# A three-stage kernel on one core: the written-out order of its first half, arranged anew

## The chip, the core and the metric

The kernel runs on one core of a Trainium2 chip. The metric is device time in microseconds (us) for one execution of the whole program, lower is better. The engines are named as the profile names them: PE (TensorE, with PEld for its weight loads), DVE (VectorE), ACT (ScalarE), POOL (GpSimd) and SP (SyncE, which here issues every DMA).

## What is computed

Three stages follow each other: a gated linear attention over 768 steps for 2 x 8 heads of width 40, then a gated feed-forward layer (320 to 1536 and back) with an RMS norm ahead of it, then a second feed-forward layer (320 to 2048 and back) with a leaky ReLU. All data is float32.

```
# attention, step t
m_new = max(f + m, i);  f_stab = exp(f + m - m_new);  i_stab = exp(i - m_new)
C = f_stab * C + i_stab * outer(v, k);  n = f_stab * n + i_stab * k
y[t] = sigmoid(o_gate) * (C @ q) / max(|n . q|, 1)
# first feed-forward
xn = x / sqrt(mean(x*x) + 1e-6) * rms_g
x = (silu(xn @ w_gate) * (xn @ w_val)) @ w_out
# second feed-forward
h = x @ w_in;  x = max(0.01*h, h) @ w_out2
```

## The kernel before

The 1536 tokens are 12 tiles T of 128 (chunk c = T // 2 of batch T % 2). The attention works chunk by chunk, with a state C carried from chunk to chunk; four groups g of three tiles each (0 to 2, 3 to 5, 6 to 8, 9 to 11) then go through the feed-forward layers, with 12 blocks f of 128 hidden columns in the first one. Weights and activations are split into a high and a low float32r half, and a product is summed from several matmuls.

Nothing is scheduled at build time. ORDER is a text of 1928 short steps, and play() emits the instructions of one step after the other. Each engine works off its own instructions strictly in that order, SP its DMAs too, so the text sets every queue. The steps that the prediction speaks of, with the line of their main instruction:

- sf, sa (L231, L232, L238): scans over the gates on DVE; id (L226): a matmul without use, which only keeps PE at work.
- fa.T.e (L258, L261): PE builds the decay rows A of tile T for the even or odd heads, in PSUM; arg.T.e (L351): ACT turns them into weights w by four exponentials. From tile 2 on, the rows come by DMA as Ab, and POOL masks them first (mask, L355).
- qk.T (L335): scores s on PE. p.T.e (L382): DVE multiplies scores and weights. av, inn, kv (L395, L405, L417): the attention's other matmuls, into one PSUM bank of tile T. eq, k, c (L359, L374, L364): POOL prepares operands of inn and kv and scales the state.
- y1, rec, yr, sq, y2, xn, xc (L450 to L492): the output gate and the norm; y2.T.1 (L479) is on POOL, xn (L488) on DVE. tp.T (L499) transposes on PE, xh.T (L503, ACT) and xl.T (L507, DVE) write tile T of X, the input of the first feed-forward layer.
- a, r, b (L536, L538, L540 and after): a weight block is converted in four steps that alternate between DVE and ACT. wA, wR, wB are the DMAs of it.
- U.g.f.h (L646): eight up matmuls of group g, block f, gate or value half h. T, E, M, S, L (L673 or L671, L678, L685 or L683, L694, L700): the activation, the products and the split of the result into sh and sl, on ACT and DVE. D.g.b.i (L718) and DW (L736): the down matmuls; K and KW: their sums into x2.

The PSUM banks of the attention, of the up matmuls, of the down sums and of the scores come from four pools of two banks each. Loads have two or three buffers, so a DMA on SP waits until its buffer is free, and those behind it wait too.

Group 1 cannot begin (U.1.0.0) before xl.5 has written the last of its tiles. U.1.0.0 is the 84th step on PE. The step DW.1.8 is the 193rd on PE.

Of the kernel before, what the change touches and what calls it, by code (L numbers as in the profile page):

```python
# [51 lines left out]
co.0.0.1 cv.0.0.1 cr cl r.1 fa.0.0 arg.0.0 sf.2.6 fa.1.1 uv.0.1 arg.1.1 fa.0.1 sa.2.6 uv.1.2 ux.0.1 co.1.0.1 wR.0
ug.2.6 id.1 co.0.1.2 arg.0.1 r.1 r.0 r.1 r.0 id.1 dn.2 dA.0.2 dq.1 r.0 ev.1.2 ux.2.6 ex.1.2 r.0 r.1 a.0 dn.1 cv.1.0.1
fa.1.0 arg.1.0 dn.0 th.0 eg.2.6 k.0 da.2 ex.2.6 a.0 k.1 qk.0 p.0.0 qk.1 a.0 p.1.0 av.0.0 p.0.1 av.0.1 abs.0 p.1.1
av.1.0 av.1.1 da.3 id.1 mask.2.1 cv.0.1.2 mask.2.0 co.0.2.6 dE.1.2 y1.0 id.1 arg.2.0 a.0 kv.0 abs.1 wR.2 r.2 mask.3.1
rec.0 wA.1 a.1 rec.1 r.2 dq.2 a.1 yr.0 id.1 mask.3.0 arg.3.0 r.2 id.1 r.2 qk.2 th.1 st.0 y1.1 de.2 dA.2.6 eq.2 ux.1.2
co.1.1.2 cv.1.1.2 cv.0.2.6 sq.0 y2.0.0 yr.1 wA.2 kv.1 dgb p.2.0 av.2.0 arg.2.1 y2.0.1 p.2.1 y2.0.2 k.2 sq.1 y2.1.0 a.2
y2.1.1 a.1 xn.0 a.2 arg.3.1 a.1 dq.3 qk.3 p.3.1 dq.4 cb.0 wB.1 a.2 xc.0 b.1 dsl y2.1.2 th.2 a.2 dr.2.6 da.4 mask.4.1
wA.4 xn.1 av.2.1 inn.2 y1.2 xc.1 id.1 st.1 abs.2 id.1 id.1 id.1 p.3.0 rec.2 tp.0 id.1 b.1 tp.1 dn.3 yr.2 dr.1.2
mask.4.0 dc.1.2 a.4 sq.2 b.1 y2.2.0 kv.2 xh.1 wR.3 th.3 de.3 dE.2.6 k.3 b.1 id.1 xh.0 xl.0 av.3.0 co.1.2.6 cv.1.2.6  # L60
xl.1 cb.1 y2.2.1 y2.2.2 r.3 qk.4 eq.3 av.3.1 inn.3 dv.1.2 xn.2 arg.4.0 xc.2 tp.2 abs.3 r.3 r.3 c.3 rec.3 dn.5 kv.3 a.4
xh.2 arg.4.1 xl.2 U.0.1.1 p.4.0 k.5 y1.3 da.5 a.4 st.3 U.0.1.0 cb.3 p.4.1 th.5 T.0.1 dn.4 th.4 mask.5.0 wA.3 yr.3 sq.3
a.4 E.0.1 mask.5.1 a.3 arg.5.1 dc.2.6 de.4 r.3 arg.5.0 y2.3.0 a.3 eq.4 M.0.1 av.4.0 av.4.1 inn.4 dq.5 qk.5 y2.3.1 y1.4
p.5.1 U.0.0.0 p.5.0 T.0.0 E.0.0 dv.2.6 U.0.0.1 M.0.0 da.6 mask.6.1 arg.6.1 de.5 wB.0 abs.4 dq.6 a.3 rec.4 mask.6.0
av.5.0 av.5.1 S.0.1 eq.5 y2.3.2 yr.4 S.0.0 inn.5 kv.5 abs.5 b.0 xn.3 rec.5 b.0 sq.4 y2.4.0 y2.4.1 arg.6.0 qk.6 L.0.1
p.6.1 U.0.2.0 p.6.0 U.0.2.1 T.0.2 E.0.2 c.2 y1.5 dq.7 b.0 c.5 st.5 qk.7 yr.5 y2.4.2 c.4 cb.5 sq.5 a.3 k.4 kv.4 id.1
xc.3 tp.3 xh.3 y2.5.0 y2.5.1 dq.8 xn.4 da.7 xc.4 M.0.2 wB.2 U.0.3.0 st.4 cb.4 y2.5.2 c.6 L.0.0 xn.5 xl.3 tp.4 xh.4
xl.4 U.0.3.1 S.0.2 xc.5 T.0.3 tp.5 xh.5 de.6 dn.6 av.6.0 E.0.3 xl.5 av.6.1 wB.3 M.0.3 L.0.2 eq.6 inn.6 abs.6 wA.5 b.0
b.3 U.1.0.0 T.1.0 E.1.0 U.1.0.1 M.1.0 U.1.1.0 da.8 U.1.2.0 b.3 mask.7.0 arg.7.0 p.7.0 dn.7 av.7.0 mask.7.1 arg.7.1
p.7.1 av.7.1 k.7 S.0.3 b.2 L.0.3 de.7 b.2 eq.7 S.1.0 b.2 inn.7 L.1.0 b.2 b.3 b.3 wB.4 rec.6 T.1.2 E.1.2 mask.8.1 a.5  # L70
# [1025 lines left out]
```

## Time and profile before

| | |
|---|---|
| times of three runs | 445.22, 447.4, 451.2 us; median 447.4 |
| span of the profiled execution | 449.2 us (inside the three runs' range, 1.8 above their median) |
| PE busy | 437.8 us, 97% |
| DVE, ACT, POOL busy | 365.8 (81%), 281.3 (63%), 102.1 us (23%) |
| chain that ended last | PE 89%, DVE 6%, ACT 2%, issue 2% |

A busy time is the time in which at least one instruction of the engine is under way. Matmuls overlap each other, so a stretch in which PE is busy need not be one in which it is fast. The column PEclk in the rows below is the granted TensorE clock, as a share of its upper level of 2.4 GHz; 0.5 is the lower level of 1.2 GHz.

### The profile page before, as it was taken

To read this page: it belongs to the slowest core of one execution; us is meant where nothing else is said; L and a number is where in the kernel's file an instruction comes from. 1 tells how busy PE (TensorE), PEld (TensorE's weight loads), DVE (VectorE), ACT (ScalarE), POOL (GpSimd) and SP (SyncE) were. 2 spreads that over 40 slices of the span, in tenths; PEclk is the share of its full clock that TensorE was granted. 3 is DMA by queue.
4 is the path that set the end of the run, shared out by engine and by line. 5 is a ranking of instruction groups with operands and counts; after the bars stand their busy time and mean duration, and the time that the engine had idled before them with its cause. 6 is when DMAs were issued, how large, how long until landed. Compare 5 with 4: busy or idle time off the path is not lost.

```text
span 449.2 us, 9736 instructions
## 1 busy us (share of the span) xinstructions
PE 437.8 (97%) x3720; PEld 415.7 (93%) x3720; DVE 365.8 (81%) x822; ACT 281.3 (63%) x709; POOL 102.1 (23%) x162
## 2 busy tenths in 40 slices
...
GB/s 267 316 265 283 251 287 119 265 232 82 248 88 77 56 0 175 78 83 0 124 1 1 1 1 0 1 1 153 30 31 76 107 47 32 31 29 31 0 2 176
DMA packets 21039, 45.47 MB, mean 101 GB/s; under 512 B 2128, under 2 KB 9168, under 8 KB 20992
## 3 DMA queue, kind: packets, MB, share of 16 engines
...
HBM read 42.79 MB, written 2.06 MB: 100 GB/s over the span
## 4 chain that ended last, share of the span: by engine, by line
PE 89%; DVE 6%; ACT 2%; issue 2%; DVEq 0%; ACTq 0%
PE h L796 13%; PE xa L718 10%; PE g L646 8%; PE v L646 8%; PE oa L969 6%; PE oa L968 6%; PE oa L967 6%; PE u L796 6%; PE xw L736 5%; PE s L335 3%; PE h L802 2%; PE h L801 2%; PE o L395 2%; PE busy L226 2%; PE o L405 1%
## 5 line engine op out<-in xcount | busy, mean ns | idle before, releaser
L969 PE MATMUL oa<-wB,xl 128*128 128x320 f32 x192 | 59.3, 309 | 0.0
L968 PE MATMUL oa<-wB,xh 128*128 128x320 f32 x192 | 59.3, 309 | 0.0
L967 PE MATMUL oa<-wB,xh 128*128 128x320 f32 x192 | 59.2, 308 | 0.0
L646 PE MATMUL g<-X,wA 128*128 128x384 f32 x256 | 50.7, 343 | 0.9 <-ACT th L671 0.4
L979 DVE TENSOR_TENSOR x<-oa,x 128x320 f32<-128x320 f32 x84 | 39.5, 484 | 14.6 <-PE oa L969 13.9
L646 PE MATMUL v<-X,wA 128*128 128x384 f32 x256 | 50.0, 339 | 0.1
L646 PEld LDWEIGHTS g<-X,wA 128*128 128x128 f32 x256 | 44.5, 189 | 2.9 <-ACT th L671 0.7
L718 PE MATMUL xa<-sh,wB 128*128 128x384 f32 x160 | 46.0, 338 | 0.0
L646 PEld LDWEIGHTS v<-X,wA 128*128 128x128 f32 x256 | 44.6, 188 | 0.7 <-DVE X L507 0.4
L578 POOL TENSOR_TENSOR sums<-w_A 128x128 f32<-128x128 f32 x8 | 3.9, 488 | 151.8 <-DVE w_A L540 146.6
L969 PEld LDWEIGHTS oa<-wB,xl 128*128 128x128 f32 x192 | 36.0, 188 | 0.1
L967 PEld LDWEIGHTS oa<-wB,xh 128*128 128x128 f32 x192 | 36.0, 188 | 0.0
L968 PEld LDWEIGHTS oa<-wB,xh 128*128 128x128 f32 x192 | 36.0, 188 | 0.0
L796 PE MATMUL h<-X,wA 128*128 128x384 f32 x144 | 32.2, 337 | 0.0
L718 PE MATMUL xa<-sl,wB 128*128 128x384 f32 x96 | 32.2, 336 | 0.0
L943 ACT ACTIVATE c<-c 128x384 f32<-128x384 f32 x48 | 25.2, 525 | 7.2 <-DVE c L840 3.4
L718 PEld LDWEIGHTS xa<-sh,wB 128*128 128x128 f32 x160 | 29.4, 188 | 0.1
L953 DVE TENSOR_TENSOR xl<-c,xh 128x384 fp32r<-128x384 f32 x48 | 26.1, 556 | 1.0 <-ACT xh L948 0.8
L948 ACT CAST xh<-c 128x384 fp32r<-128x384 f32 x48 | 24.3, 513 | 2.9 <-PE oa L968 2.2
L351 ACT ACTIVATE w<-Ab,aeu 128x128 f32<-128x128 f32 x80 | 25.3, 392 | 0.6 <-POOL Ab L355 0.6
L796 PEld LDWEIGHTS h<-X,wA 128*128 128x128 f32 x144 | 25.0, 188 | 0.1
L479 POOL TENSOR_TENSOR sm<-sm,mhalf 128x1 f32<-128x1 f32 x12 | 8.0, 663 | 65.0 <-DVE sm L477 65.0
...
## 6 DMA issues: line engine op xcount, KB each, us to landing
...
```

Of the source, the lines that this page charges most:

```text
L351: A.activation(w[:, j], src, AF.Exp, scale=-1.0, bias=col)
L646: PE.matmul(dst, a, x, start=(i == 0), stop=(i == len(seq) - 1))
L718: PE.matmul(xa, w, x, start=(k == 0), stop=(k == len(seq) - 1))
L736: PE.matmul(xas["w", g, i], a, x, start=(f == NE and k == 0), stop=(f == NF - 1 and k == len(seq) - 1),)
L796: PE.matmul(dst, x, y, start=first and j == 0, stop=j == 2, skip_group_check=not first)
L943: A.activation(t, src, AF.Prelu, alpha=0.01)
L948: A.copy(v["h"], v["t"])
L953: V.tensor_tensor(v["l"], v["t"], v["h"].bitcast(F32), op=ALU.subtract)
L967: PE.matmul(oa, v["h"][:, ts], wb[:, 0:DM], start=m == 0, stop=False)
L968: PE.matmul(oa, v["h"][:, ts], wb[:, DM:], start=False, stop=False)
L969: PE.matmul(oa, v["l"][:, ts], wb[:, 0:DM], start=False, stop=m == 1)
L979: V.tensor_tensor(dst, oas[k, p, i], dst, op=ALU.add)
```

## The change

Only the text ORDER differs: its first 1028 steps stand in another order, the last 900 (from S.1.11 on) are the same. Each of the 1928 steps occurs as often as before; no function and no size is touched. The text takes one line more, so that the code below it is one line further down in the changed kernel (L646 is L647 there). The first line of either text:

```diff
-id.1 id.1 id.1 id.1 did cr id.1 id.1 dfg dig id.1 id.1 id.1 wR.1 dq.0 ms id.1 sf.0.1 sa.0.1 sf.1.2 id.1 sa.1.2 wA.0
+id.1 id.1 id.1 id.1 id.1 cl wR.1 r.1 id.1 id.1 id.1 id.1 dfg ms dig sf.0.1 r.1 did cr cr co.0.0.1 id.1 id.1 sa.0.1
```

**The start on SP and DVE.** DVE before, from its first instruction on (x is the space of the gates; raw_R and w_R belong to the first weight block, wgr):

```order
L231 SCALAR_TENSOR_TENSOR x_91<-x_91 16x128
L232 TENSOR_TENSOR x_91<-x_91 16x128
L238 SCALAR_TENSOR_TENSOR x_91<-x_91 16x128
L231 SCALAR_TENSOR_TENSOR x_91<-x_91 16x128
L232 TENSOR_TENSOR x_91<-x_91 16x128
L237 COPY x_91<-x_91 16x1
L238 SCALAR_TENSOR_TENSOR x_91<-x_91 16x128
L252 COPY aeu<-pt_0_152 128x16
L536 TENSOR_SCALAR w_R_160<-raw_R_130 128x256
```

The same place now:

```order
L537 TENSOR_SCALAR w_R_124<-raw_R_122 128x256
L232 SCALAR_TENSOR_TENSOR x_91<-x_91 16x128
L233 TENSOR_TENSOR x_91<-x_91 16x128
L541 SCALAR_TENSOR_TENSOR w_R_124<-raw_R_122,w_R_124 128x256
L239 SCALAR_TENSOR_TENSOR x_91<-x_91 16x128
L232 SCALAR_TENSOR_TENSOR x_91<-x_91 16x128
L233 TENSOR_TENSOR x_91<-x_91 16x128
L238 COPY x_91<-x_91 16x1
L239 SCALAR_TENSOR_TENSOR x_91<-x_91 16x128
```

The first two steps of the conversion r.1 stand around the first scan. SP before begins with the constants, the two gate inputs and then this weight block; now:

```order
L527 DMA raw_R_122<-wgr 128x512
L994 DMA x_91<-fg 16x768
L994 DMA x_91<-ig 16x768
L995 DMA consts<-cst 128x256
L315 DMA nat_173<-nat 128x968
L996 DMA sel<-cst 16x136
L527 DMA raw_R_176<-wgr 128x512
L527 DMA raw_A_222<-wgv 128x1024
L310 DMA qkt_224<-qk 128x1024
```

The weight block goes first, the constants fourth, and the first scores' operand qkt ninth instead of fifth.

**The first scores on PE.** Before, the last of the four fa (A rows) stands just ahead of qk.0 (s is its output):

```order
L226 LDWEIGHTS const-bfloat16-1.0
L226 MATMUL busy<-const-bfloat16-1.0 128x512
L258 MATMUL A_0_246<-consts_r 128x512
L261 MATMUL A_0_246<-x_91,consts 128x128 x4
L335 MATMUL s_0_270<-qkt_132 128x128
L335 MATMUL s_1_271<-qkt_132 128x128
```

Now qk.0 follows the third fa and two small transposes:

```order
L259 MATMUL A_1_189<-consts_r 128x512
L262 MATMUL A_1_189<-x_91,consts 128x128 x4
L249 MATMUL pt_0_195<-consts,x_91 128x16
L249 MATMUL pt_1_230<-consts,x_91 128x16
L336 MATMUL s_0_232<-qkt_224 128x128
L336 MATMUL s_1_233<-qkt_224 128x128
```

The fourth fa has gone behind qk.1, and arg.1.1, which reads it on ACT, has moved back too.

**The end of group 1's attention on DVE and POOL.** DVE before, up to the write of tile 5 (xl.5, the last row; sm are the norm's columns, tp the transposed tiles):

```order
L481 TENSOR_SCALAR sm_1038<-sm_1038 128x1
L482 TENSOR_SCALAR sm_1038<-sm_1038 128x1
L483 TENSOR_TENSOR sm_1038<-sm_1038 128x1
L700 TENSOR_TENSOR sl_0_1168<-th_0_933,sh_0_1012 128x384
L488 SCALAR_TENSOR_TENSOR xn_1170<-y_1093,sm_1038,gb 128x320
L507 TENSOR_TENSOR X<-tp_1135,X 128x3x128
L507 TENSOR_TENSOR X<-tp_1173,X 128x3x128
L678 SCALAR_TENSOR_TENSOR th_3_1191<-th_3_1191,g_3_1152 128x384
L507 TENSOR_TENSOR X<-tp_1193,X 128x3x128
```

Now:

```order
L482 TENSOR_SCALAR sm_1030<-sm_1030 128x1
L483 TENSOR_SCALAR sm_1030<-sm_1030 128x1
L484 TENSOR_TENSOR sm_1030<-sm_1030 128x1
L701 TENSOR_TENSOR sl_0_1134<-th_0_961,sh_0_1067 128x384
L508 TENSOR_TENSOR X<-tp_1137,X 128x3x128
L489 SCALAR_TENSOR_TENSOR xn_1163<-y_1044,sm_1030,gb 128x320
L508 TENSOR_TENSOR X<-tp_1117,X 128x3x128
L679 SCALAR_TENSOR_TENSOR th_3_1161<-th_3_1161,g_3_1101 128x384
L508 TENSOR_TENSOR X<-tp_1181,X 128x3x128
```

One of the three writes of X has moved ahead of xn.5. POOL at that place before, from the norm's step y2.5.1 on:

```order
L479 TENSOR_TENSOR sm_1038<-sm_1038,mhalf 128x1
L364 TENSOR_TENSOR C_95<-C_95,gdec 104x164
L359 TENSOR_TENSOR eb_1198<-eb_1198,qkt_964 128x512
L355 AFFINE_SELECT Ab_1146<-Ab_1146 128x4x128 x2
L374 TENSOR_TENSOR Kt_100<-nat_1321,aeu 128x4x40 x2
```

and now:

```order
L480 TENSOR_TENSOR sm_1030<-sm_1030,mhalf 128x1
L360 TENSOR_TENSOR eb_1144<-eb_1144,qkt_1089 128x512
L375 TENSOR_TENSOR Kt_99<-nat_1157,aeu 128x4x40 x2
L365 TENSOR_TENSOR C_95<-C_95,gdec 104x164
L356 AFFINE_SELECT Ab_1278<-Ab_1278 128x4x128 x2
```

The state's scaling c.6 has moved behind eq.6 and k.6, and the two masks of tile 7 behind all of them.

Over the whole first part, the same 83 steps stand on PE ahead of U.1.0.0 in both texts, and the same 192 ahead of DW.1.8. On DVE, 121 steps end with xl.5 before and 119 now; the two that have gone behind it are the first two of the conversion b.0.

## Rows read from the trace of the kernel before

**Rows 1.** Windows: stage (from:to, length), busy us of each engine, clock, DMA.
```profile
core 0: us, PE busy (x) PEld busy (x) DVE busy (x) ACT busy (x) POOL busy (x), PEclk, DMA share, GB/s
0.00:9.40 9.40, 8.62 (x32) 4.23 (x32) 5.41 (x14) 4.01 (x10) 3.16 (x13) 1.00 0.73 246
9.40:47.48 38.08, 35.06 (x516) 26.53 (x516) 28.73 (x82) 25.99 (x83) 16.07 (x23) 0.55 0.93 288
47.48:73.65 26.17, 23.53 (x447) 20.86 (x445) 25.36 (x59) 18.02 (x55) 14.21 (x22) 0.95 0.81 260
73.65:211.26 137.61, 136.72 (x1310) 132.40 (x1307) 106.54 (x252) 82.66 (x224) 32.88 (x47) 1.00 0.37 113
211.26:449.20 237.94, 233.82 (x1425) 231.66 (x1424) 199.79 (x420) 150.60 (x341) 35.77 (x58) 1.00 0.13 41
```

**Rows 2.** Timeline of PE: tp.5 and the first up matmuls of group 1.
```profile
70.73 0.64 PE L499 MATMUL tp<-consts,xn 128*128 128x128 f32 x3 [2.49 <-DVE X L507]
73.65 2.00 PE L646 MATMUL g<-X,wA 128*128 128x384 f32 x8
75.48 1.55 PE L646 MATMUL v<-X,wA 128*128 128x384 f32 x8
76.87 3.05 PE L646 MATMUL g<-X,wA 128*128 128x384 f32 x16
```

**Rows 3.** Windows of DVE alone, cut at p.1.1, p.2.1, xl.2 and xl.5.
```profile
0.00:21.23 21.23, 12.82 (x32) 0.72 0.83 294
21.23:30.82 9.59, 7.89 (x23) 0.50 0.93 291
30.82:48.00 17.18, 13.95 (x43) 0.63 0.94 255
48.00:72.45 24.45, 23.64 (x57) 0.97 0.84 272
```

**Rows 4.** Waits of DVE until 74 us: total, times, longest.
```profile
DVE x L231 <- DMA x<-fg: 3.3, 1, 3.3
DVE w_R L540 <- ACT raw_R L538: 2.3, 1, 2.3
DVE w L382 <- PE s L335: 1.6, 2, 1.1
```

**Rows 5.** Timeline of DVE: xn and yr, each once long and once short.
```profile
66.95 3.17 DVE L488 SCALAR_TENSOR_TENSOR xn<-y,sm,gb 128x320 f32<-128x320 f32 x1
64.76 0.54 DVE L488 SCALAR_TENSOR_TENSOR xn<-y,sm,gb 128x320 f32<-128x320 f32 x1
49.76 1.58 DVE L464 TENSOR_TENSOR y<-y,sm 128x320 f32<-128x320 f32 x1
63.09 0.52 DVE L464 TENSOR_TENSOR y<-y,sm 128x320 f32<-128x320 f32 x1
```

**Rows 6.** Timeline of POOL beside the long xn.
```profile
66.79 0.58 POOL L364 TENSOR_TENSOR C<-C,gdec 104x164 f32<-104x164 f32 x1 [1.08 <-DMA raw_B<-wo]
67.32 1.28 POOL L359 TENSOR_TENSOR eb<-eb,qkt 128x512 f32<-128x512 f32 x1
68.56 1.22 POOL L355 TENSOR_SCALAR_AFFINE_SELECT Ab<-Ab 128x512 f32<-128x512 f32 x2
```

**Rows 7.** POOL groups until 74 us: k (Kt) and its mean.
```profile
L374 POOL TENSOR_TENSOR Kt<-nat,aeu 128x160 f32<-128x160 f32 x14 | 7.2, 537 | 13.4 <-DVE aeu L252 3.6 <-PE tp L499 3.6 <-PE o L417 3.2
```

**Rows 8.** Timeline, the start: second gate input, first weight block, first p.
```profile
4.16 0.28 DVE L232 TENSOR_TENSOR x<-x 16x128 f32<-16x128 f32 x1 [0.44 <-DMA x<-ig]
5.50 0.44 ACT L538 ACTIVATE raw_R<-raw_R 128x256 f32<-128x256 f32 x1 [1.70 <-DMA raw_R<-wgr]
17.55 0.69 DVE L382 TENSOR_TENSOR w<-s,w 128x512 f32<-128x512 f32 x1 [0.56 <-PE s L335]
```

**Rows 9.** Timeline of DVE: the two steps of b.0 ahead of xl.5.
```profile
58.75 0.32 DVE L536 TENSOR_SCALAR w_B<-raw_B 128x320 uint32<-128x320 uint32 x1
59.77 0.44 DVE L540 SCALAR_TENSOR_TENSOR w_B<-raw_B,w_B 128x320 uint32<-128x320 uint32 x1
```

More of the change, by code (lines that the diff above doesn't have):

```diff
@@ L50 @@
 ORDER = """
-id.1 id.1 id.1 id.1 did cr id.1 id.1 dfg dig id.1 id.1 id.1 wR.1 dq.0 ms id.1 sf.0.1 sa.0.1 sf.1.2 id.1 sa.1.2 wA.0
[L52 to L70, printed above, removed]
```

210 lines of the change are left out of this document (115 added, 95 removed).

## The prediction

> **What bounds the kernel now.** The first view is the row of windows by stage, cut at three places of PE's order: where U.1.0.0 starts (73.65), where DW.1.8 starts (211.26), and earlier where the first up matmul starts (47.48). In the last two stages PE is busy 136.72 of 137.61 us and 233.82 of 237.94 us at the full granted clock, 1.00 [rows 1]. There the kernel is bound by PE's own work; no order of the same matmuls can take more than the 0.9 us of idle time from the second last stage, and the last one keeps its order. What an order can win lies in the first 73.65 us.
>
> In that part PE isn't the bound. From 9.40 to 47.48 its granted clock is 0.55, mostly the lower level of 1.2 GHz, and DVE is busy 28.73 of 38.08 us [rows 1]. From 47.48 to 73.65 DVE is busy 25.36 of 26.17 us. U.1.0.0 at 73.65 is held up by the transposes ahead of it: tp.5 waits 2.49 us for DVE [rows 2]. So the second view is DVE alone, cut at four steps whose last one, xl.5, ends at 72.45: busy 12.82 + 7.89 + 13.95 + 23.64 = 58.3 us, idle 8.4 + 1.7 + 3.2 + 0.8 = 14.1 us [rows 3]. The third view says what the idle time waited for: 3.3 us for the first gate input, 2.3 for ACT's first step on the second weight block, 1.6 for the scores [rows 4]. The fourth is DVE's timeline, where some busy time is a wait in disguise. An xn takes 0.54 us at 64.76 and 3.17 at 66.95; a yr 0.52 at 63.09 and 1.58 at 49.76 [rows 5]. During the long xn, POOL runs four instructions end to end, from 66.79 to 69.78 [rows 6].
>
> **The change, part by part.** PE runs the same 83 steps ahead of U.1.0.0 and the same 109 from there to DW.1.8; the last part isn't touched. So the sum has three terms: the time at which U.1.0.0 starts, 137.61 us behind it plus what may newly stall, and 237.94 us as before [rows 1]. DVE sets the first.
>
> *Work of DVE until xl.5.* The same steps less the two of b.0, 0.32 + 0.44 us [rows 9]; they overlap their neighbours a little, so 0.6 us are gained.
>
> *First segment, to p.1.1 (21.23 us, 8.4 idle).* The first weight block, raw_R, now goes ahead of the gate inputs. Before, it reached ACT at 5.50, 1.34 us after the second gate input reached DVE at 4.16 [rows 8]; I take this difference as its share of the queues. The constants, which went first, now follow, and give some of it back: the first scan starts 0.7 to 1.4 us later, I take 1.0. In return the 2.3 us behind ACT [rows 4] go: ACT had three exponential groups ahead of that step, and now the conversion stands ahead of them. Some 0.3 us of a similar wait come back behind the first scan. p.0.0 started at 17.55 after a wait for its scores [rows 8]. Now qk.0 no longer waits for the fourth fa; but its operand is ninth on SP instead of fifth, and the fourth fa, now behind qk.1, holds arg.1.1 and p.1.1. So I leave the waits for scores at their 1.6 us [rows 4]. DVE has 27 steps up to p.1.1 instead of 23; the four are the first two of r.2 and two column copies, by their durations in this trace 0.8 us. Sum: +1.0 - 2.3 + 0.3 + 0.8 = -0.2; p.1.1 ends at about 21.0.
>
> *Second segment (9.59 us, 1.7 idle).* DVE's work through p.2.0, the later of the two p now, is 0.4 us more than before in this segment; sq.1, th.2 and sq.0 stand on ACT ahead of arg.2.0, so the idle time stays or grows. I take 0.4 us longer than before: the end is at 31.0 instead of 30.82.
>
> *Third segment, to xl.2 (17.18 us, 3.2 idle).* The two segments before have taken 1.2 us of work from this one; and tiles 0 and 1 are now handled as a pair, with other work between an instruction and what it needs from ACT or POOL. I take 1.2 us off the work and 1.2 of the 3.2 us of waits: xl.2 at 31.0 + 14.8 = 45.8 instead of 48.0.
>
> *Fourth segment, to xl.5 (24.45 us).* The 0.6 us of b.0 go. Of the time lost beside POOL, the two long rows hold 2.63 + 1.06 = 3.7 us [rows 5]. At the end of it, POOL now has eq.6 and the two halves of k.6 behind y2.5.1: 1.28 + 2 x 0.54 = 2.4 us [rows 6, 7]; c.6 and the masks come later. DVE's three short sm rows pass 0.6 us of that, and the next one, L.0.0, then stands where xn stood. The wait is about 1.8 instead of 2.6 us. For the other long row I see no change. xl.5 at 45.8 + 24.45 - 0.6 - 0.8 = 68.9, to which I add 0.5 for waits that a tighter queue shows anew: 69.4 instead of 72.45, 3.0 us earlier.
>
> The Trainium skill (SBUF — State Buffer, "Who interferes with whom") says that a DVE instruction with two SBUF inputs and a POOL instruction that reads SBUF share an interface, and that the one that starts first holds it to its end. The long xn agrees and goes further, since DVE got no turn between the four instructions; by the rule as it stands, with one POOL instruction waited for, L.0.0 would lose 0.7 us, and the sum would be 1.1 us shorter.
>
> *Behind U.1.0.0.* PE's steps are four halves of up matmuls at 1.39 us each (75.48 to 76.87 [rows 2]), then D.0.0.0, which needs L.0.3 and all of b.3. DVE has 14 instructions from b.0 to the end of b.3, some 6.5 us, PE 5.6 us, kv.6 and three quarters of D.0.0.0 before it reads the last operand. The margin is about 1 us, so I add 0.5 us for a stall there. After the pools are closed, the new order starts U.3.0.0 directly behind U.3.1.1, in the bank that the first Silu has to free; before, such a wait was part of the 0.9 us of idle time, and I add 0.3. The first up matmul of group 1 ran at 1.83 us instead of 1.39 after PE's pause [rows 2]; a shorter pause would save part of it, and I count nothing.
>
> Sum against the profiled execution: 449.2 - 3.0 + 0.8 = 447.0, so -2.2 us. Its span is 1.8 us above the median of the three runs; against the median, 447.4 - 2.2 = 445.2, rounded to 445.0.
>
> Bounds: if none of the idle time behind the first gate input goes and the start costs its 1.4 us, the term is +1.4; if a block like that at 66.95 comes twice, +2.6 more: +4.0. If half of the 14.1 - 3.3 us of idle time and the 3.7 us beside POOL go, it is -9.1.
>
> **The rivals.** *Gain eaten up.* DVE's queue gets shorter at one place and waits at another: waits for ACT and for PE at the lower clock move with the order, and the start costs 1.0 us for certain. Then U.1.0.0 stays within 1 us of 73.65, and the time is 447 to 449. For it speaks that DVE's work is the same but for 0.6 us; against it, the 2.3 us wait that clearly goes.
>
> *Slower.* PE stalls behind U.1.0.0. D.0.0.0 has about 1 us of margin. A POOL instruction like eb or a mask pair beside the conversions of b.0, b.2 and b.3 would cost DVE 1.3 to 3 us; PE would wait, its clock would fall as it did in the pause ahead of 73.65, and the next matmuls would run 0.4 us longer per eight [rows 2]. The price is 3 to 5 us, so that with the early gain of 3.0 gone the time is 449 to 452. It decides once the stall exceeds 3 us; to be slower by over 2%, the same would have to recur in the attention of groups 2 and 3, against which speaks that DVE is busy only 106.54 of 137.61 us there [rows 1].
>
> *Much faster.* Idle time and POOL's blocks go by more than half: up to -9.1 us by the bounds above, and with PE's pause of 2.5 us and the slow matmuls behind it gone as well, -11 or -12: 436 to 439. For it speaks that 14.1 us of DVE's idle time lie there [rows 3]; against it, that PE at the lower clock and ACT lie on the same chains, and that 3.3 us are the wait for the first load.
>
> *The change does nothing.* Excluded as such: the rows of order differ at every place shown. That a different order takes the same time is the first rival.
>
> **How the numbers follow.** The forecast (441.5 to 447) gets 0.50, the gain eaten up 0.22, the stalls 0.14, much faster 0.14 (of which a little below 2%). The range from 439.5 to 451.0 leaves out most of the much faster case and the end of the stalls, about 2 in 10 together, and also holds a scatter like that of the runs shown (445.22 to 451.2). 2% is 9 us, about what a measurement of this kernel can tell from no change: faster by over 2% (below 438.5) 0.11, slower by over 2% (above 456.3) 0.06, within 0.83.
>
> **What the profile of the changed kernel would show.** Right: U.1.0.0 at 70 to 71.5, xl.2 at 45 to 47, the first scan at 4.0 to 4.7, no 2.3 us wait of w_R for ACT, at the end of group 1's attention a long DVE row of 2 to 2.6 us on L.0.0 in place of the 3.17 us xn, and 137.5 to 139 us between U.1.0.0 and DW.1.8 at a granted clock near 1.00. Wrong: U.1.0.0 before 66 or after 74, a stall of over 2 us in PE behind it, or a last stage that differs from 237.9 us by more than 1.

## The result and the profile after

The changed kernel takes 451.62 us (median of 20 runs, one of them, at 1441.85, far out), the kernel before 449.03 us on the same chip (20 runs): a ratio of 1.0064, with a 95% interval of 1.0037 to 1.0091. The prediction was 445.0 us in a range of 439.5 to 451.0. The time went the other way, by 2.6 us, and out of the range by 0.6. Against the bound of 2% it is no change.

Three things about times, which hold for all that follows. A run's time is its span plus 1.8 us (the profiled execution of after: span 452.9, time 454.73). Executions of one kernel lie 6 to 11 us apart (443.03 to 452.34 for the kernel before in one group of runs), so one trace says little about a microsecond in the total. And the ratios leave out executions more than 1.5% above the fastest of the same kernel, which beside before_again, after_again, e_ids_tab, b_pause, final and g_move_again takes away half of those of the kernel before, so that for these the medians of all executions count.

The forecast was worked out from a median of 447.4 us of three runs. The 20 runs beside the changed kernel give 449.03, so 1.6 of the 6.6 us between 445.0 and 451.62 lie in that base.

The executions of after fall into two kinds. Beside each time stands the mean granted clock of that execution. Ten of the 19 (without the one far out) have 0.974 to 0.985 and take 451.61 to 454.73 us, median 453.1; nine have 0.965 to 0.973 and take 448.85 to 450.72, median 449.75, near the kernel before. A higher clock with a longer time looks odd; the trace, which is of the first kind (0.974, 454.73 us), shows how it comes about (PE alone: stretch, length, busy us, clock, DMA):

```profile
9.40:27.04 17.64, 17.64 (x222) 1.00 0.87 310
30.45:54.35 23.90, 19.92 (x283) 0.50 0.91 253
```

The first record of the clock in this trace is at 27.04 us, at the upper level, and time without a record counts as 1.00 in the column. Yet PE's matmuls take the longer times until then (2.08 us for 16 score matmuls at 14.72 and at 16.94, 1.16 at 28.28). In after_again, of the second kind, the first record of the upper level is at 3.71 us.

The windows of after by stage, cut at the same steps of PE as [rows 1]:

```profile
0.00:9.40 9.40, 7.91 (x22) 3.81 (x22) 5.07 (x17) 4.41 (x11) 3.15 (x13) 1.00 0.73 225
9.40:51.48 42.08, 37.44 (x525) 29.18 (x527) 30.68 (x77) 24.59 (x77) 18.99 (x28) 0.75 0.84 265
51.48:76.36 24.88, 24.02 (x445) 21.23 (x445) 20.57 (x57) 17.98 (x56) 10.45 (x17) 0.94 0.63 188
76.36:215.46 139.10, 137.68 (x1311) 132.07 (x1307) 109.20 (x257) 82.36 (x227) 31.92 (x46) 1.00 0.40 127
215.46:452.90 237.44, 233.84 (x1425) 231.64 (x1424) 199.29 (x418) 149.99 (x341) 34.92 (x58) 1.00 0.13 41
```

U.1.0.0 starts at 76.36 instead of 73.65, the stage behind it takes 139.10 instead of 137.61 us, and the last one 237.44 instead of 237.94. The larger part of the loss is made ahead of the first up matmul (51.48 instead of 47.48); from there to U.1.0.0 1.3 us of it come back.

DVE alone, cut at the ends of the same steps as [rows 3] (p.1.1; the later p of tile 2, now p.2.0; xl.2; xl.5), and its longest waits until 76 us, as [rows 4]:

```profile
0.00:23.66 23.66, 14.21 (x35) 1.00 0.87 307
23.66:34.31 10.65, 7.58 (x24) 0.82 0.38 106
34.31:50.19 15.88, 13.78 (x34) 0.50 1.00 290
50.19:76.18 25.99, 20.58 (x57) 0.92 0.66 191
```

```profile
DVE w L383 <- ACT w L352: 6.3, 6, 3.9
DVE w_R L537 <- DMA raw_R<-wgr: 4.0, 1, 4.0
DVE sm L459 <- ACT sm L445: 3.2, 3, 2.4
```

The 2.3 us behind ACT's first conversion step are gone, as forecast. In their place DVE waits 3.9 us for the weights w of p.0.0, and 2.4 for abs.0. In the last segment it is busy for only 20.58 of 25.99 us: DVE, which set the pace there before (23.64 of 24.45), no longer does.

The timeline of PE at the transposes and the first up matmuls of group 1, as [rows 2] (start, duration, engine, line, operation, output and input, their size, number of instructions, and in brackets the idle time ahead and what ended it):

```profile
74.53 0.55 PE L500 MATMUL tp<-consts,xn 128*128 128x128 f32 x3
...
76.36 1.66 PE L647 MATMUL g<-X,wA 128*128 128x384 f32 x8
77.85 1.55 PE L647 MATMUL v<-X,wA 128*128 128x384 f32 x8
```

tp.5 has no 2.49 us pause ahead of it any more, and U.1.0.0 follows xl.5 (ends 76.18) within 0.2 us.

Where one trace is so uncertain, the other traces help. Three have the order of before up to U.1.0.0, and three that of after:

| us | p.1.1 ends | later p.2 ends | xl.2 ends | xl.5 ends | U.1.0.0 | U.1.0.0 to DW.1.8 |
|---|---|---|---|---|---|---|
| before | 21.21 | 30.82 | 48.02 | 72.48 | 73.65 | 137.61 |
| before_again | 21.18 | 30.52 | 45.54 | 71.87 | 72.05 | 138.06 |
| h1_late | 21.11 | 29.80 | 46.65 | 70.55 | 71.92 | 138.57 (order of after) |
| after | 23.64 | 34.31 | 50.19 | 76.18 | 76.36 | 139.10 |
| after_again | 22.90 | 33.25 | 48.05 | 72.50 | 72.68 | 138.62 |
| h2_early | 23.81 | 34.49 | 49.33 | 73.99 | 74.17 | (order of before) |

By the means of three traces each, p.1.1 is 2.3 us late, U.1.0.0 1.9 us (74.4 against 72.5), and the stage behind it takes 0.9 us more (138.8 against 137.8). The sum of 2.8 fits the medians' 2.6. The trace on which the prediction rests was the latest of the three at U.1.0.0.

### The profile page after: what moved, and what is told of

It reads as the page before. It is cut to its first block, busy times and chain, and to the rows that moved or that the text cites. A ratio compares the mean times of both kernels' runs of the same rounds, so it can differ in the third digit from the quotient of the medians.

```text
span 452.9 us, 9733 instructions
## 1 busy us (share of the span) xinstructions
PE 440.9 (97%) x3719; PEld 417.9 (92%) x3720; DVE 364.8 (81%) x822; ACT 279.3 (62%) x709; POOL 99.4 (22%) x162
## 4 chain that ended last, share of the span: by engine, by line
PE 92%; DVE 3%; ACT 2%; issue 1%; DMA 1%; DVEq 0%
PE h L797 13%; PE v L647 10%; PE g L647 10%; PE xa L719 9%; PE oa L970 6%; PE oa L969 6%; PE oa L968 6%; PE u L797 6%; PE xw L737 5%; PE s L336 3%; PE h L803 2%; PE h L802 2%; PE o L396 2%; PE A L262 2%; PE o L418 1%; PE o L406 1%
## 5 line engine op out<-in xcount | busy, mean ns | idle before, releaser
L647 PE MATMUL g<-X,wA 128*128 128x384 f32 x256 | 50.7, 341 | 1.4 <-ACT th L672 1.3
L647 PE MATMUL v<-X,wA 128*128 128x384 f32 x256 | 51.5, 346 | 0.0
L647 PEld LDWEIGHTS g<-X,wA 128*128 128x128 f32 x256 | 44.2, 188 | 3.0 <-ACT th L672 1.6
L647 PEld LDWEIGHTS v<-X,wA 128*128 128x128 f32 x256 | 45.7, 192 | 0.4
L383 DVE TENSOR_TENSOR w<-s,w 128x512 f32<-128x512 f32 x24 | 16.3, 685 | 8.1 <-ACT w L352 7.0
```

The costliest lines, as they stand in the source:

```text
L647: PE.matmul(dst, a, x, start=(i == 0), stop=(i == len(seq) - 1))
```

## The experiments

Every kernel is a text ORDER; the diffs show its steps. "Before" in a ratio is always the kernel before, run beside it.

### Halves of the order

h2_early is the order of after up to U.1.0.0 and then the steps that are left in the order of before; h1_late is the reverse.

> The changed kernel's order up to and with U.1.0.0, and then the steps that are left in the order of before. Theory: the loss comes from two parts, 2.7 us ahead of U.1.0.0 and 1.5 us behind it (DW.1.8 is 4.2 us late, the last stage 0.5 us shorter). Then this kernel has U.1.0.0 at 76 to 77 us, the stretch from U.1.0.0 to DW.1.8 at 137.5 to 138 us, and a time of 1.0050 to 1.0060 times that of before. Rival one: all of the loss is made in the first part, and the 1.5 us behind U.1.0.0 are only its echo (loads and buffers that are late): then the time is 1.007 to 1.009. Rival two: the first part's loss is made up by PE's slack behind it: below 1.003.

460.9 us against 447.77, ratio 1.028 (1.0218 to 1.0342). U.1.0.0 stands at 74.17, but the stage behind it takes 147.4 us (DW.1.8 at 221.61). The waits of PE from 74 to 100 us:

```profile
PE g L646 <- DVE th L678: 2.4, 1, 2.4
PE o L405 <- POOL eb L359: 1.6, 1, 1.6
PE o L395 <- DMA nat<-nat: 1.2, 1, 1.2
```

None of the expectations holds. By these waits, the order of before behind U.1.0.0 needs loads and conversions of tile 7 and b.0 that the new first part hasn't made yet, so this kernel says nothing on the first part's own price.

> The order of before up to and with U.1.0.0, and then the steps that are left in the changed kernel's order. Theory of two separate losses: U.1.0.0 at 73 to 74 us, 138.5 to 139.5 us from there to DW.1.8, the wait of U.3.0.0 for the first Silu of 1.0 to 1.5 us is still there, and the time is 1.002 to 1.004 times that of before. Rival (all of the loss is made ahead of U.1.0.0): 0.999 to 1.001, and the stretch is back at 137.6 us.

449.03 against 447.77 us, ratio 1.0019 (0.9982 to 1.0057); U.1.0.0 at 71.92, 138.57 us from there, the wait of U.3.0.0 for the Silu 1.3 us. By the trace the late part costs 0.5 to 1.0 us by itself; the ratio alone can't tell this from nothing.

### Executions of the same order

> The kernel before, unchanged, for a second trace of it. U.1.0.0 came 1.7 us earlier in the kernel whose order is that of before up to this step (71.92 against 73.65). Expected of both theories: 0.997 to 1.003 times the kernel before. If executions of the same order differ by the clock of PE, the fa groups or the scores run fast over another stretch here and U.1.0.0 differs from 73.65 by up to 2 us; if not, every time up to U.1.0.0 lies within 0.5 us of the first trace.

449.39 us (12 runs; before itself 450.17 with 29 runs beside it), ratio 1.0028 (0.9978 to 1.0079) for the same kernel. U.1.0.0 at 72.05, 1.6 us earlier than in the first trace, though p.1.1 ends within 0.03 us of it. In between PE's matmuls run fast over another stretch: tile 4's scores take 1.16 us here (at 40.45) and 2.08 there (at 42.10).

> The changed kernel, unchanged, for a second trace and a comparison beside the others on one chip. Expected: 1.004 to 1.009 times the kernel before. If the pause of PE at 4.8 us is what keeps its clock low, all four fa groups run at about 2.07 us per eight matmuls here too; if that was chance of one execution, some of them run at 1.15.

452.03 us against 450.17, ratio 1.0122 (1.006 to 1.0184), medians of all 1.004. U.1.0.0 at 72.68, 3.7 us earlier than in after's first trace. None of the first three fa groups runs at 1.15 us (1.74, 2.07, 2.07), as the theory has it, but the clock wasn't kept low: its upper level stands from 3.71 to 7.12 us in this trace and falls for the most part on id and on PE's pause of 1.20 us ahead of co.0.0.1.

### PE's clock in the first 14 us

PE's timeline at the start, of the kernel before, where fa.0.0 (L258 and L261) begins at 5.77:

```profile
0.78 4.85 PE L226 MATMUL busy<-const-bfloat16-1.0 128*128 128x512 bf16 x11 [0.78 <-PEq L1087]
5.56 0.28 PE L248 MATMUL pt<-consts,x 16*128 16x16 f32 x1
5.77 0.66 PE L258 MATMUL A<-consts_r 128*128 128x512 f32 x1
6.36 1.15 PE L261 MATMUL A<-x,consts 16*128 16x128 f32 x8
7.44 0.50 PE L258 MATMUL A<-consts_r 128*128 128x512 f32 x1
7.88 1.15 PE L261 MATMUL A<-x,consts 16*128 16x128 f32 x8
```

and of after, where the lines stand one further down:

```profile
5.49 0.26 PE L249 MATMUL pt<-consts,x 16*128 16x16 f32 x1 [0.73 <-DVE w_R L541]
5.68 1.03 PE L227 MATMUL busy<-const-bfloat16-1.0 128*128 128x512 bf16 x2
6.44 0.76 PE L259 MATMUL A<-consts_r 128*128 128x512 f32 x1
7.13 2.07 PE L262 MATMUL A<-x,consts 16*128 16x128 f32 x8
9.13 0.80 PE L259 MATMUL A<-consts_r 128*128 128x512 f32 x1
9.86 2.07 PE L262 MATMUL A<-x,consts 16*128 16x128 f32 x8
```

The same eight matmuls take 1.15 us there and 2.07 here, nearly the factor two between the two levels of the clock, 2.4 and 1.2 GHz. A group costs 1.5 us (7.44 to 8.96, where the third begins) or 2.7 us (6.44 to 9.13). Ahead of the groups PE had no pause in before and one of 0.73 us in after.

```diff
@@ e_ids: the changed kernel, ahead of and behind co.0.0.1, and two id from 22 to 25 us
-co.0.0.1
-id.1 id.1
+id.1 id.1 id.1 id.1
+co.0.0.1
```

> The changed kernel, with four of the matmuls without use (id) moved ahead of co.0.0.1 in PE's queue: the two behind it and two from between 22 and 25 us. Reason: in the kernel before, PE has work without a pause from 1.58 us on, and three of the four fa groups run at 1.15 us per eight matmuls; in the changed kernel PE pauses for 0.73 us at 4.77, and all four run at 2.07 us. Theory (the pause kept PE at its lower clock, and PE sets the times of the first scores): at least two fa groups run at about 1.15 us, p.1.1 ends at 20.5 to 22.5 us instead of 23.64, U.1.0.0 starts 1 to 2.5 us earlier, and the time is 0.995 to 0.998 times that of the changed kernel (1.001 to 1.004 times before). Rival (the first 24 us are held by the late constants and the late fa.1.1 alone, or the lost time is hidden later): p.1.1 within 0.5 us of 23.64, the time that of the changed kernel.

449.38 us against 447.77, ratio 1.0025 (0.999 to 1.006), less than after's 1.0064, though the two intervals overlap. Two fa groups run at 1.15 us although the first begins only at 6.56; p.1.1 ends at 21.21, U.1.0.0 starts at 69.72. The theory gets what it asked for, and more at U.1.0.0, in this trace. A part of it may come from the two id that no longer stand ahead of kv.0, as in g_move below. (In before two of the four fa groups run at 1.15 us, not three.)

```diff
@@ b_pause: the kernel before, two of the eleven id ahead of co.0.0.1
 ms
-id.1
 sf.0.1 sa.0.1 sf.1.2
-id.1
 sa.1.2
...
 av.1.1
+id.1 id.1
```

> The kernel before, with two of the eleven id ahead of co.0.0.1 moved behind av.1.1, so that PE pauses for some 0.8 us ahead of the first fa, as it does in the changed kernel; nothing else is moved. Theory (the pause alone keeps PE at its lower clock for the fa groups, which take 2.07 instead of 1.15 us): qk.0 and p.1.1 come 2 to 3 us later (p.1.1 at 23 to 24.5 instead of 21.21), U.1.0.0 1 to 2.5 us later than in the kernel before, and the time is 1.003 to 1.006 times before. Rival (the clock at the start is not on the path, DVE and ACT are): p.1.1 within 1 us of 21.2 and the time within 0.2% of before.

449.42 us against 450.17, medians of all 0.998 (ratio 1.0058, 1.001 to 1.0107, in the group where the identical kernel got 1.0028). In the trace nothing followed from it: PE went from the nine id to co.0.0.1 at 4.50 without a pause, and the first two fa groups ran at 1.15 us. But three of the 12 executions have a mean clock of 0.976 to 0.992 and take 450.56 to 452.98 us, like the first kind of after. The pause may have come about in them; none of the three was traced.

The traces side by side; the six that are left out (f_both, b_fa_late, g_move twice, g_fill, final) have no such pause, a first record at 4.59 to 6.69 us and no execution of the first kind. The last column counts the executions that are surely of that kind, with a mean clock of 0.974 or more and a time above 450 us; every other execution with such a clock takes 448.4 us or less.

| trace | PE's pause ahead of the fa, us | first record of the upper level, us | first three fa groups (eight matmuls), us | U.1.0.0 | of the first kind |
|---|---|---|---|---|---|
| before | none | 6.14 | 1.15, 1.15, 1.95 | 73.65 | 0 of 145 (all groups of runs) |
| before_again | none | 4.80 | 1.15, 1.27, 2.07 | 72.05 | 0 of 12 |
| h1_late | none | 6.74 | 1.26, 1.15, 1.61 | 71.92 | 0 of 12 |
| f_dma | none | 4.86 | 1.15, 1.25, 2.07 | 69.99 | 0 of 12 |
| e_ids | none | 6.39 | 1.15, 1.15, 2.07 | 69.72 | 0 of 12 |
| e_ids_tab | 0.58 | 4.45 | 1.16, 2.07, 2.07 | 71.11 | 0 of 12 |
| b_pause | none | 4.22 | 1.15, 1.15, 2.07 | 71.41 | 3 of 12 |
| f_fa | 0.72 | 5.45 | 1.15, 1.51, 2.07 | 72.68 | 5 of 12 |
| after_again | 1.20 | 3.71 | 1.74, 2.07, 2.07 | 72.68 | 2 of 6 |
| e_kv | 1.54 | 3.66 | 2.07, 2.07, 2.07 | 75.75 | 2 of 6 |
| after | 0.73 | 27.04 | 2.07, 2.07, 2.07 | 76.36 | 10 of 19 |
| h2_early | 0.89 | 26.29 | 2.07, 2.07, 2.07 | 74.17 | 3 of 6 |
| g_cst | 1.10 | 27.23 | 2.07, 2.07, 2.07 | 75.96 | 2 of 12 |
| b_dma | 0.53 | 27.23 | 2.07, 2.07, 2.07 | 75.02 | 2 of 12 |

So it isn't the lateness of the first fa that costs the upper level: in e_ids and f_fa it begins at 6.56 and 6.26, hardly earlier than in after (6.44), and runs fast. Executions of the first kind came only where PE pauses ahead of the fa, or has two id fewer there (b_pause), and not in all of these: after and f_fa have the same start, yet the level rises at 27.04 in the one trace and at 5.45 in the other.

### The start, put back and put in

```diff
@@ f_dma: the changed kernel's first steps
-id.1 id.1 id.1 id.1 id.1 cl wR.1 r.1 id.1 id.1 id.1 id.1 dfg ms dig sf.0.1 r.1 did cr cr
-co.0.0.1 id.1 id.1 sa.0.1 fa.1.0 sf.1.2 sa.1.2
+id.1 id.1 id.1 id.1 id.1 cl did cr cr dfg dig id.1 id.1 id.1 id.1 wR.1 ms sf.0.1
+co.0.0.1 id.1 id.1 sa.0.1 fa.1.0 sf.1.2 sa.1.2 r.1 r.1
```

> The changed kernel, with the constants first on SP again, then the two gate inputs, then the first weight block, whose first two steps go behind sa.1.2 on DVE. Theory (the late constants hold the first fa to 6.3 to 6.6 us, instead of 4.7 to 5.8 with the order of before, and most of the short fast stretch of PE's clock then falls on the pause and on matmuls without use): the first scan at 3.2 to 3.4 us, fa.1.0 at 5.0 to 5.9, at least one more fa group at 1.15 us, p.1.1 1.2 to 2.2 us earlier than in the changed kernel (21.3 to 22.2), U.1.0.0 1 to 2 us earlier (mean of its traces 74.4), time 0.996 to 0.998 times that of the changed kernel. Rival (the weight block's conversion, now behind, takes the gain back on DVE): p.1.1 within 0.7 us of 23.4.

449.13 us against 449.30, ratio 1.0012 (0.9982 to 1.0041). The first scan starts at 3.27, the first fa at 5.45, and two groups run fast:

```profile
5.45 0.47 PE L259 MATMUL A<-consts_r 128*128 128x512 f32 x1
5.85 1.15 PE L262 MATMUL A<-x,consts 16*128 16x128 f32 x8
6.94 0.49 PE L259 MATMUL A<-consts_r 128*128 128x512 f32 x1
7.36 1.25 PE L262 MATMUL A<-x,consts 16*128 16x128 f32 x8
```

p.1.1 ends at 20.84, U.1.0.0 starts at 69.99. Putting the start back takes away the whole loss, as far as the times can show it.

```diff
@@ b_dma: the kernel before's first steps
-id.1 id.1 id.1 id.1 did cr id.1 id.1 dfg dig id.1 id.1 id.1 wR.1 dq.0 ms id.1 sf.0.1 sa.0.1
+id.1 id.1 id.1 id.1 wR.1 r.1 id.1 id.1 dfg dig id.1 id.1 id.1 ms id.1 sf.0.1 r.1 did cr dq.0 sa.0.1
```

(the two r.1 go from their places further down)

> The kernel before with the start of the changed one alone: the first weight block ahead of the gate inputs on SP, the constants behind them, and the first two steps of this block's conversion around the first scan on DVE. Theory (this start makes the first fa 0.7 to 1 us late and leaves the fast stretch of PE's clock to matmuls without use): the first scan at 4.0 to 4.6 us, the first fa at 6.2 to 6.6 instead of 4.7 to 5.8, p.1.1 1 to 2 us later than the 20.4 to 21.2 of that order, U.1.0.0 1 to 2 us later than its mean of 72.2, time 1.002 to 1.005 times before. Rival (the start does harm only in the new order, since DVE here has the conversion's steps out of the way): p.1.1 at most 1 us later, U.1.0.0 in 71.4 to 73.7, time within 0.2% of before.

451.29 us against 449.12, ratio 1.0037 (1.0004 to 1.0069): the start alone makes the kernel before 2.2 us slower by the medians, 0.2 to 3.1 by the interval. PE ran without a pause until 5.96 and then waited 0.53 us for the cast of the constants:

```profile
6.48 0.79 PE L258 MATMUL A<-consts_r 128*128 128x512 f32 x1 [0.53 <-ACT consts_r L994]
7.20 2.07 PE L261 MATMUL A<-x,consts 16*128 16x128 f32 x8
9.21 0.80 PE L258 MATMUL A<-consts_r 128*128 128x512 f32 x1
9.93 2.07 PE L261 MATMUL A<-x,consts 16*128 16x128 f32 x8
```

All the fa groups are slow; p.1.1 ends at 24.60, 3.4 us late, U.1.0.0 starts at 75.02. This trace is of the first kind, one of two sure ones among 12. The other ten executions have a median of 450.81 us, still 1.7 above before, and none of them was traced.

```diff
@@ g_cst: the changed kernel
-cl wR.1 r.1
+cl did wR.1 r.1
...
-r.1 did cr cr
+r.1 cr cr
```

> The changed kernel with one step moved: the load of the constants goes first on SP, ahead of the weight block; gate inputs and DVE's order stay. If the late constants alone are what f_dma took away: the first fa at 5.4 to 5.9 us although the first scan stays at 4.3 to 5.2, p.1.1 at 21.0 to 22.0, U.1.0.0 1 to 2 us earlier than the changed kernel's, and the time as that of f_dma, 0.999 to 1.003 times before. If the late gate inputs (the first scan) are: the first fa at 6.2 to 6.6, p.1.1 at 22.9 to 23.8, the time 1.004 to 1.008 times before.

452.15 us against 449.12, ratio 1.0073 (1.0047 to 1.0099), as the changed kernel. With the constants first, the weight block still stands ahead of the gate inputs, on SP and on DVE, and the scans come even later:

```profile
4.32 0.29 DVE L537 TENSOR_SCALAR w_R<-raw_R 128x256 uint32<-128x256 uint32 x1 [4.32 <-DMA raw_R<-wgr]
4.65 0.41 DVE L232 TENSOR_TENSOR_SCAN x<-x 16x128 f32<-16x128 f32 x1
5.53 0.28 DVE L233 TENSOR_TENSOR x<-x 16x128 f32<-16x128 f32 x1 [0.47 <-DMA x<-ig]
5.74 0.41 DVE L541 SCALAR_TENSOR_TENSOR w_R<-raw_R,w_R 128x256 uint32<-128x256 uint32 x1
```

The first fa begins at 6.84. So it isn't the constants alone: it is the weight block ahead of the gate inputs. Whether its load or its two steps on DVE weigh more wasn't separated.

### The fourth fa, and the kv ahead of the abs

```diff
@@ f_fa: the changed kernel
+fa.1.1 arg.1.1
 qk.0 p.0.0
+p.0.1
...
-p.0.1
+p.1.1
...
-fa.1.1
```

(also arg.0.0 ahead of arg.0.1, and av.1.1 behind av.1.0)

> The changed kernel, with its fourth fa group (fa.1.1) and arg.1.1 put back ahead of qk.0, arg.0.0 ahead of arg.0.1, and the four p of the first two tiles (and av.1.1) in the order that the scores then come in. In three traces with the changed order, p.1.1 ends at 22.9 to 23.8 us, in four with the order of before at 20.4 to 21.2. Theory (fa.1.1 behind qk.1 puts arg.1.1 and p.1.1, some 2 us of ACT and DVE, behind PE's last matmul of this stage): p.1.1 ends at 22.0 to 22.9, 0.7 to 1.2 us earlier than in the changed kernel with the same clock at the start, U.1.0.0 0.5 to 1.5 us earlier than the 72.7 to 76.4 of the changed kernel, time 0.997 to 0.999 times that of the changed kernel. Rival (PE's own time sets p.1.1, since the fa and qk at the lower clock have no pause between them): the end of p.1.1 within 0.4 us of 23.2.

452.22 us against 449.30, ratio 1.007 (1.0035 to 1.0106): no gain. p.1.1 ends at 20.86, but ACT's abs.0 then waits for kv.0, which comes off PE no earlier:

```profile
25.17 0.18 ACT L445 ACTIVATE sm<-o 128x8 f32<-128x8 f32 x1 [4.17 <-PE o L418]
```

rec.0 starts at 25.38, between 25.00 and 26.08 in the traces of after, although the first two fa groups run at 1.15 and 1.51 us here and PE has only one pause from the first fa to kv.0, of 0.74 us at 21.5. The theory that fa.1.1 behind qk.1 costs the time falls: what is gained at p.1.1 is lost again up to rec.0, and the time is no better.

```diff
@@ b_fa_late: the kernel before
-fa.1.1 uv.0.1 arg.1.1 fa.0.1
+uv.0.1 fa.0.1
...
 qk.1
+fa.1.1
...
 abs.0
+arg.1.1
 p.1.1
```

> The kernel before with one feature of the changed one: fa.1.1 behind qk.1 on PE, and arg.1.1 just ahead of p.1.1. Theory (this feature makes p.1.1 late, and what is late there stays late up to U.1.0.0): p.1.1 ends at 22.3 to 23.5 us instead of 20.4 to 21.2, U.1.0.0 1 to 2 us later than the 71.4 to 73.7 of the four traces with that order, time 1.002 to 1.005 times before. Rival (the delay at p.1.1 is made up behind it, because DVE has other work there): p.1.1 as late, but U.1.0.0 in 71.4 to 73.7 and a time within 0.2% of before.

449.34 us against 449.30, ratio 1.0014 (0.9984 to 1.0044). p.1.1 is late, at 22.64, rec.0 by 0.9 us, and U.1.0.0 at 71.92 isn't late at all: the rival holds.

f_both has both edits, that of f_dma and that of f_fa.

> Both edits together: the start of f_dma and the fa.1.1 of f_fa. If the two causes add up: p.1.1 at 20.3 to 21.5 us, U.1.0.0 at 70 to 72, the stretch behind it 138.5 us as in the changed kernel, and the time 0.993 to 0.997 times that of the changed kernel, so 0.998 to 1.002 times before. If PE alone sets p.1.1, f_both is as f_dma.

449.79 us against 449.30, ratio 1.0027 (0.9995 to 1.0059); p.1.1 at 19.52, U.1.0.0 at 71.07. The second edit adds nothing to f_dma.

```diff
@@ e_kv: the changed kernel
-kv.0 arg.1.1
+arg.1.1
...
 abs.0
+kv.0
```

(and likewise kv.1, kv.3 and kv.4)

> The changed kernel, with kv.0, kv.1, kv.3 and kv.4 moved directly behind abs.0, abs.1, abs.3 and abs.4, as they stand in the kernel before. An abs on ACT reads the PSUM bank that the kv of its tile writes, so an abs behind the kv in the text waits for it: 2.10 us on ACT for abs.0, 1.62 for abs.3 and 1.34 for abs.4 in the changed kernel, and rec.0 on DVE waits 2.44. Theory (these waits are on the path to xl.5): rec.0 at 24.5 to 25.5 us instead of 26.08, U.1.0.0 1 to 2 us earlier, the time 0.995 to 0.998 times that of the changed kernel. Rival (they move the wait to the next step): U.1.0.0 within 0.5 us of 76.36, the time within 0.2% of the changed kernel.

453.37 us against 447.77, ratio 1.0145 (1.0088 to 1.0202): no gain, and by the medians 1.3 to 1.8 us slower than the changed kernel. rec.0 comes at 23.87, 2.2 us earlier, as the theory has it, but kv.1 now waits for abs.1, and behind it on PE the scores of tile 2 are late:

```profile
28.56 1.05 PE L418 MATMUL o<-nat,Kt 128*64 128x41 f32 x16 [2.17 <-ACT sm L445]
...
31.16 2.08 PE L336 MATMUL s<-qkt 40*128 40x128 f32 x16
```

They run at 28.28 in after, in 1.16 us. The slower pace is the clock: in this trace it reads 0.50 from 7.07 to 48.03 us. The later p of tile 2 ends at 35.41 instead of 34.31.

### PE's pause near 30 us

In the new order two column transposes hold both banks of their pool, and an id behind them waits for one: PE pauses from 29.8 to 32.6 us, and until 45 or 54 us its matmuls take the longer times. U.0.1.1, the first row of each timeline, shows which, in after:

```profile
51.48 3.06 PE L647 MATMUL v<-X,wA 128*128 128x384 f32 x8
54.38 1.55 PE L647 MATMUL g<-X,wA 128*128 128x384 f32 x8
```

and in after_again:

```profile
47.90 1.76 PE L647 MATMUL v<-X,wA 128*128 128x384 f32 x8
49.49 1.55 PE L647 MATMUL g<-X,wA 128*128 128x384 f32 x8
```

```diff
@@ g_move: the kernel f_dma, two id of 20 to 23 us and the steps around qk.2; g_fill has thirteen id here
-id.1 y2.1.1 co.0.2.6 cv.0.2.6 id.1 qk.2 p.2.1 dr.1.2 co.1.2.6 id.1 cv.1.2.6
+y2.1.1 qk.2 id.1 id.1 id.1 id.1 id.1 co.0.2.6 cv.0.2.6 co.1.2.6 p.2.1 dr.1.2 cv.1.2.6
```

> The kernel f_dma with two of its id from the stretch 20 to 23 us moved behind qk.2, together with the three that stand around qk.2 and the two column transposes co.0.2.6 and co.1.2.6: qk.2 first, then five id, then both co. In f_dma an id behind co.1.2.6 waits for a bank of these transposes, and PE pauses from 25.7 to 29.1 us. Expected: rec.0 0.4 to 0.9 us earlier than in f_dma (22.57), because kv.0 comes earlier on PE; U.1.0.0 0 to 1 us earlier than 69.99; time 0.998 to 1.000 times that of f_dma.

447.66 us against 449.12, ratio 0.997 (0.9942 to 0.9999). rec.0 at 21.45, 1.1 us earlier than in f_dma, and the later p.2 as much. U.1.0.0 is at 71.70 in this trace, where U.0.1.1 runs in 3.12 us; f_dma's trace had 1.74.

> As g_move, with eight further id behind qk.2 (eight matmuls without use more than the reference needs), so that PE has no pause of more than 1.5 us between 24 and 31 us. Theory (the pause at 26 to 29 us costs the upper level of the clock, which comes back only at 42 to 54 us, and with it 2 to 3 us in some executions): the matmuls of 31 to 45 us run at the upper level (tile 3's scores, 16 matmuls, at 1.16 us instead of 2.08), U.0.1.1 1 to 2.5 us earlier than in g_move, time 0.994 to 0.998 times that of g_move. Rival (the clock falls there in any case, as it did in the kernel before without such a pause): scores at 2.08 us, time within 0.2% of g_move.

449.56 us against 449.12, ratio 0.9995 (0.9961 to 1.0028). The scores of tile 3 do run in 1.16 us (at 32.65), but the transposes stand behind the thirteen id and hold up p.2.1 by 1.5 us, and tile 4's scores take 1.90 us again. Keeping PE at work there brought nothing over g_move.

### Behind U.1.0.0

After close, U.3.0.0 waits for the first Silu and its table load, in the order U.3.2.0, U.3.1.0, U.3.1.1, U.3.0.0:

```profile
167.50 2.95 PE L647 MATMUL g<-X,wA 128*128 128x384 f32 x16
170.29 1.55 PE L647 MATMUL v<-X,wA 128*128 128x384 f32 x8
173.10 1.66 PE L647 MATMUL g<-X,wA 128*128 128x384 f32 x8 [1.27 <-ACT th L672]
```

```diff
@@ e_ids_tab: the kernel e_ids
 a.9
+T.3.1
 a.9 a.9 a.8 a.9
-T.3.1
```

> The changed kernel with the four id moved to the start as in the run e_ids, and with T.3.1 (the first Silu behind close, with its table load) moved ahead of two steps of a.9, one of a.8 and one more of a.9, so that the cast of a.9, which waits 0.76 us for DVE, no longer stands ahead of it on ACT. Theory (the loss behind U.1.0.0 is U.3.0.0's wait of 1.2 us for this Silu): the wait falls below 0.4 us, U.1.0.0 to DW.1.8 takes 137.3 to 137.9 us instead of 138.56, and the time is 0.9975 to 0.9985 times that of e_ids, 0.999 to 1.001 times before. Rival (another wait follows at once, since the conversions of a.8 and a.9 come later): the stretch stays at 138.3 to 139 us and the time that of e_ids.

449.93 us against 450.17, ratio 1.0075 (1.0036 to 1.0114), medians of all 0.999. The wait falls to 0.53 us, and 0.85 us come back in front of U.1.8.0, whose weights' last steps a.8 now stand behind T.3.1 on ACT: 138.43 us, the rival.

```diff
@@ final: the kernel g_move
+U.3.2.1
 U.3.0.0
...
-U.3.2.1
...
+U.3.3.1
 U.1.8.0
...
-U.3.3.1
```

> The kernel g_move, with the value halves U.3.2.1 and U.3.3.1 moved ahead of U.3.0.0 and U.1.8.0 on PE, so that PE has one more up half to run while U.3.0.0 waits for the first Silu behind close, and one more while a.8's conversion ends. Theory (the loss behind U.1.0.0 is this wait): no wait of U.3.0.0 over 0.3 us, U.1.0.0 to DW.1.8 in 137.0 to 137.8 us instead of 138.57, time 0.997 to 0.998 times that of g_move, about 0.994 to 0.996 times before. Rival (as when T.3.1 was moved, the wait only goes to the next step): 138.3 to 138.8 us and the time of g_move.

447.40 us against 449.71: medians of all 0.995, means 447.36 and 449.15 (12 and 23 runs), ratio 1.0012 (0.9978 to 1.0046). The stretch is 137.40 us, 1.2 shorter, with one wait of 0.5 us left:

```profile
71.43:208.83 137.40, 136.88 (x1310) 131.83 (x1307) 108.83 (x257) 82.44 (x227) 32.96 (x46) 1.00 0.41 129
```

> The kernel g_move, unchanged, beside the run final, for a second trace and a second comparison. Expected: 0.994 to 1.000 times before; rec.0 at 21 to 22 us, U.1.0.0 at 68.5 to 71.7 us, 138.3 to 138.8 us from there to DW.1.8.

448.58 us against 449.71, medians of all 0.997, ratio 0.9968 (0.9935 to 1.0001); rec.0 at 21.40, U.1.0.0 at 71.65, 138.63 us behind it. By their medians (447.40, 447.66, 448.58) final and g_move lie 3.0 to 4.6 us below the changed kernel (451.62 to 452.03), and probably a little below the kernel before.

## Why the prediction was wrong

**The step that failed: the start, "I take 1.0".** The first segment was to end at 21.0, 0.2 us earlier. It ends at 22.9 to 23.8. The delay of the first scan itself was right (4.29 instead of 3.31). What it costs was taken for DVE's queue alone. But in after PE has no pause from 5.49 to 29.8 us, so up to kv.0 its own matmuls are the bound, with four fa groups and two sets of scores end to end; and their pace isn't fixed. The first three fa groups take 8.0 us in after (6.44 to 14.46) and 5.4 in before (5.77 to 11.14). The times place the loss in the start: f_dma takes it away and b_dma brings 2.2 us of it (0.2 to 3.1). The way from the start to the loss is shown in part. The new start makes PE pause ahead of the fa, and ten of its 19 executions are, by their clock and time, like the traced one, in which no upper level comes before 27 us: these take 453.1 us, the others 449.75. f_dma and e_ids, which both close this pause, have no such execution among 12 each, and e_ids leaves the weight block first on SP and DVE. But b_dma and g_cst are also slow in executions that aren't surely of this kind, so it isn't the whole account. The prediction read the column of the clock in [rows 1], 1.00 up to 9.40, and never the length of the fa.

**The 2.3 us behind ACT** went, as forecast, but DVE waited for w instead: an idle time of an engine that isn't the bound is worth nothing.

**Second segment, +0.4.** It was +1.0 in the trace and +1.4 by the means (10.6 against 9.2). abs.0 stands behind kv.0 in the text, reads the same bank and waits for it, and DVE's rec.0 waits 2.4 us for abs.0; the prediction named no wait of ACT for PE. Turning the pair around only shifts the wait (e_kv), and taking two id from ahead of kv.0 gives 1.1 us (g_move).

**Third segment, -2.4.** -1.3 in the trace (15.88 instead of 17.18), -1.2 by the means (15.2 against 16.4). Half, and the trace's 17.18 was the longest of the three.

**Fourth segment, -0.8.** Nothing by the means (25.0 against 24.9). The long row of 3.17 us [rows 5] vanished outright; L.0.0 took 0.55 us. POOL's last row beside it, in after's timeline:

```profile
71.47 0.89 POOL L375 TENSOR_TENSOR Kt<-nat,aeu 128x160 f32<-128x160 f32 x2
```

and DVE's row:

```profile
72.45 0.55 DVE L701 TENSOR_TENSOR sl<-th,sh 128x384 fp32r<-128x384 f32 x1
```

POOL's three instructions ended at 72.36, just ahead of it. So the 1.8 us priced there were not lost, and yet nothing came of it, since DVE had 5.4 us of idle time in this segment. The Trainium skill (SBUF — State Buffer, "Who interferes with whom") on the interface that DVE and POOL share was therefore not put to the test at this place.

**U.1.0.0 against xl.5.** 0.2 us behind it instead of 1.2, a gain of 0.7 by the means that was not forecast.

**Behind U.1.0.0, +0.8.** Right in size (0.9), wrong in place. The 0.5 us at D.0.0.0 didn't come. The wait for the Silu, forecast at 0.3 above before, is 1.27 us against the 0.9 us of idle time of all this stage in before; final, which fills it, gets 1.2 us back.

**The rivals.** "Slower" was priced behind U.1.0.0, where the larger loss isn't; that its 449 to 452 us hold the measured 451.62 is luck. "Gain eaten up" had the right sentence, "the start costs 1.0 us for certain", and too small a price: p.1.1 is 2.3 us late by the means.

**Were the other steps sound?** f_dma, the new order with the start put back, ends p.1.1 at 20.84, the later p.2 at 30.81, xl.2 at 45.62 and xl.5 at 69.81; the forecast had 21.0, 31.0, 45.8 and 69.4. That they agree so closely is partly luck: the three traces in the order of before lie 2.5 us apart at xl.2. It is one trace, and its time of 448.1 us lies 1.0 below the median of its kernel. And the -2.2 us forecast against one trace of before can't be seen in the times either: f_dma is at 1.0012.

**Open.** Which of the weight block's load and its two DVE steps delays the start; why one start gives both kinds of execution; and how PE's clock decides between 44 and 54 us in one and the same order.
